# Splitting the first loads of q and k in two, with conversion, transposes and copies of the parts overlapped, in a fused sigmoid attention and SwiGLU kernel

## The chip, the cores and the metric

The kernel runs on one core of a Trainium2 chip. The metric is the device time of one execution in microseconds (us); lower is better. A kernel is compared with the kernel before only in the same rounds on the same chip.

## The reference

```python
def _attn_ref(q, k, v):                    # (8, 12, 448, 64) each
    S = q.shape[2]
    scores = q @ k.transpose(0, 1, 3, 2) / np.sqrt(q.shape[-1]) - np.log(S)
    return (1.0 / (1.0 + np.exp(-scores))) @ v

def _moe_ref(x, w_gate, w_val, w_out):     # x (3584, 768), d_ff 1536
    g = x @ w_gate
    return (g * (1.0 / (1.0 + np.exp(-g))) * (x @ w_val)) @ w_out
# reference = _moe_ref of the attention's output, heads joined, (3584, 768) float32
```

## The kernel before

The attention is cut into 24 tiles n of four heads, each into seven chunks c of keys. For a tile, q and k are loaded as float32, converted to bfloat16, transposed (for the first tiles on TensorE, by way of PSUM), multiplied into scores, put through a sigmoid on ScalarE (ACT), and multiplied with v ("PV"); three VectorE (DVE) instructions evacuate PV. Four PSUM tiles of two banks go round as a ring. The loads of v and of the weights convert to float16 on the way and are all issued by GpSimd (POOL).

```python
def load(n, which, eng=None):
    st = stg.tile([128, 2, S], FP32, tag="stg", name=f"st{which}_{n}")
    (eng or nc.sync).dma_start(out=st, in_=src_of(n, which))
    qkv_st[(n, which)] = st
# ... cut: cast(n, which, eng, lo, hi) converts chunks lo to hi of a loaded tile
load(0, 1, nc.scalar)                                  # first k
for n, which in ((0, 0), (1, 0), (1, 1), (2, 0), (2, 1), (3, 0), (3, 1)):
    load(n, which)                                     # SyncE's queue
# ... cut: sigmoid table
for i in range(9):                                     # warm-up of TensorE
    nc.tensor.matmul(out=ring[i % 4][:, i // 4 % 2, :], lhsT=warm[:, :128], rhs=warm, start=True, stop=True)
cast(0, 0, V)
cast(0, 1, nc.scalar, 0, 2)
cast(0, 1, G, 2, C)
trans_pe(0, ((0, 0, C), (1, 0, 2)), (V, nc.scalar))    # both into one PSUM tile
chunk(0, 0)                                            # scores and sigmoid
chunk(0, 1)
trans_pe(0, ((1, 2, C),))
cast(1, 0, G)
cast(1, 1, V)
load_v(0)                                              # on GpSimd's queue
w_load("g", 0)
# ... cut: more loads on GpSimd, chunks (0, 2) to (0, 4), trans_pe(1)
cast(2, 0, V)
cast(2, 1, V)
cast(3, 0, V)
cast(3, 1, V)
# ... cut: chunks (0, 5) to (1, 2)
pv(0)
# ... cut
for i, at in enumerate(((6, 4), (7, 0), (7, 4), (8, 0))):
    begin[at].append(lambda i=i: w_load("o", i))       # output weights
```

## Time and profile before

| | value | where it is read |
|---|---|---|
| time | 429.3 us (429.28 to 429.45) | three executions |
| span of the profiled execution | 426.6 us | page, first line |
| TensorE busy | 97% of the span | page, part 1 |
| first sigmoid starts | 7.95 us | timeline of ACT |
| v of tile 0 lands | 13.51 us | load records, issued 7.49, 6.0 us to landing |
| PV of tile 0 starts | 14.63 us | timeline of TensorE (PE) |
| last of the 21 head sigmoids starts | 26.32 us | timeline of ACT |

The timelines count from the first instruction; "landing" is the moment at which a load's semaphore tells that it is complete. Of the 10.7 us in which PE is idle, 5.6 lie in the first 30 us, where the change acts, and 4.4 after 394 us. From the last of the head's 21 sigmoids on, PE is dense, and every trace of this study without a new wait repeats that remainder to within 0.3 us (426.6 - 26.3 = 400.3 us here). The start of that sigmoid is therefore the figure by which to compare traces.

### The profile page before, as it was taken

How to read it: one execution, taken by the hardware profiler on the slowest of the kernel's cores; microseconds unless marked ns; L12 is line 12 of the kernel's file. 1: busy time of each engine (PE TensorE's matmuls, PEld its weight loads, DVE VectorE, ACT ScalarE, POOL GpSimd, SP SyncE). 2: the span in 40 equal slices, each digit the busy share in tenths (PEclk: the TensorE clock that was granted, in tenths of full speed). 3: DMA queues.
4: the chain of work that ended last, by engine and by line, in shares of the span. 5: the costliest groups of instructions: out<-in, count | busy, mean ns of one | idle time of the engine just before them, and what ended most of it. 6: DMA issues, size and time to landing. Idle time of an engine off the chain costs nothing.

```text
span 426.6 us, 7903 instructions
## 1 busy us (share of the span) xinstructions
PE 415.9 (97%) x3261; PEld 217.6 (51%) x3261; DVE 204.9 (48%) x337; ACT 211.9 (50%) x291; POOL 117.5 (28%) x167
## 2 busy tenths in 40 slices
PE   6899999999999999999999999999999999999995
PEld 2544544545555444545555544544555545555663
DVE  2726656555324555555323556555433356555322
ACT  4966885654624755656433755746433642222000
POOL 5564346401637346000345545000221100000000
PEclk8799999999999999999999999999999999999999
DMA  8999999995699997500298996600162300000234
GB/s 301 231 277 211 210 190 208 177 247 99 152 218 174 194 174 178 115 0 2 71 229 169 226 193 164 120 0 2 23 131 71 81 0 2 0 2 0 55 94 111
DMA packets 57796, 54.38 MB, mean 127 GB/s; under 512 B 35680, under 2 KB 52448, under 8 KB 57760
## 3 DMA queue, kind: packets, MB, share of 16 engines
q0 software_dynamic: 20896, 39.20, 40.9%
q1 hardware_dynamic: 36512, 14.13, 20.3%
q8 instruction: 25, 0.41, 0.4%
q10 hardware_dynamic: 352, 0.56, 0.4%
q14 instruction: 11, 0.09, 0.1%
HBM read 47.19 MB, written 11.01 MB: 136 GB/s over the span
## 4 chain that ended last, share of the span: by engine, by line
PE 91%; ACT 3%; DVE 2%; issue 1%; DMA 1%; ACTq 0%; DVEq 0%
PE ps_D L256 50%; PE ps_D L296 26%; PE ps_D L197 8%; PE ps_D L228 7%; ACT pt L215 2%; DMA st<-in_q_dram 1%; PE ps_D L171 1%; DVE t L273 1%; ACT s L271 1%; ACT pt L212 1%; DVE T L180 0%; DVE hT L277 0%; DVE xT L237 0%; DVE xT L245 0%; ACT xT L243 0%
## 5 line engine op out<-in xcount | busy, mean ns | idle before, releaser
L215 ACT ACTIVATE pt<-ps_D,sb_t 128x896 f16<-128x896 f32 x148 | 140.3, 1014 | 84.4 <-PE ps_D L197 84.2
L256 PE MATMUL ps_D<-xT,wg 128*128 128x448 f16 x576 | 126.9, 353 | 0.9 <-ACT pt L215 0.5
L256 PE MATMUL ps_D<-xT,wv 128*128 128x448 f16 x576 | 126.4, 352 | 0.0
L296 PE MATMUL ps_D<-wo,hT 128*128 128x384 f16 x672 | 111.8, 326 | 0.0
L273 DVE TENSOR_TENSOR t<-ps_D,s 128x448 f16<-128x448 f32 x96 | 59.9, 624 | 92.3 <-ACT s L271 92.0
L271 ACT ACTIVATE s<-ps_D 128x448 f16<-128x448 f32 x96 | 52.7, 549 | 90.6 <-PE ps_D L256 80.1
L296 PEld LDWEIGHTS <-hT 128*128 128x128 f16 x672 | 64.8, 98 | 46.4 <-issue 4.3
L256 PEld LDWEIGHTS <-wg 128*128 128x128 f16 x576 | 53.7, 98 | 58.5 <-issue 12.4
L256 PEld LDWEIGHTS <-wv 128*128 128x128 f16 x576 | 56.4, 98 | 52.8 <-issue 0.3
L327 DVE TENSOR_SCALAR osb<-ps_D 128x384 f32<-128x384 f32 x55 | 30.7, 558 | 74.2 <-PE ps_D L296 71.0
L277 DVE SCALAR_TENSOR_TENSOR hT<-ps_D,t 128x448 f16<-128x448 f32 x96 | 60.0, 625 | 10.4 <-DVE t L273 0.5
L337 POOL DMA_DIRECT2D out_dram<-osb x42 | 22.4, 537 | 146.1 <-DVE osb L327 146.1
L149 POOL CAST c<-st 128x896 bf16<-128x896 f32 (+1 forms) x42 | 38.8, 936 | 63.1 <-issue 29.6
L197 PE MATMUL ps_D<-T,T 64*64 64x448 bf16 x672 | 47.4, 367 | 2.3 <-ACT T L180 1.1
L228 PE MATMUL ps_D<-pt,v 64*64 64x448 f16 x672 | 36.2, 351 | 0.3 <-ACT pt L215 0.3
L197 PEld LDWEIGHTS <-T 64*64 64x64 bf16 x672 | 16.3, 107 | 25.9 <-issue 18.2
L237 DVE CAST xT<-ps_D 128x448 f16<-128x448 f32 x24 | 15.0, 625 | 29.8 <-PE ps_D L228 23.0
L245 DVE CAST xT<-ps_D 64x448 f16<-64x448 f32 x46 | 28.6, 622 | 0.7
L228 PEld LDWEIGHTS <-v 64*64 64x64 f16 x672 | 19.9, 108 | 13.0 <-issue 1.5
L212 ACT ACTIVATE pt<-ps_D,sb_t 128x448 f16<-128x448 f32 x40 | 23.0, 631 | 0.0
L140 POOL DMA_DIRECT2D v<-in_v_dram x24 | 17.7, 738 | 0.1
L135 POOL DMA_DIRECT2D st<-in_k_dram x20 | 14.7, 736 | 3.1 <-DMA wv<-in_moe_w_val_dram 3.1
(25 smaller groups left out, 59.6 us busy)
## 6 DMA issues: line engine op xcount, KB each, us to landing
st<-in_q_dram POOLq DMA_DIRECT2D x20, 448.0 KB, 4.8
st<-in_k_dram POOLq DMA_DIRECT2D x20, 448.0 KB, 7.0
out_dram<-osb POOLq DMA_DIRECT2D x42, 192.0 KB, 3.1
v<-in_v_dram POOLq DMA_DIRECT2D x24, 224.0 KB, 8.3
wg<-in_moe_w_gate_dram POOLq DMA_DIRECT2D x4, 576.0 KB, 14.4
wv<-in_moe_w_val_dram POOLq DMA_DIRECT2D x4, 576.0 KB, 14.6
wo<-in_moe_w_out_dram POOLq DMA_DIRECT2D x4, 576.0 KB, 14.7
out_dram<-osb SPq DMA_DIRECT2D x12, 192.0 KB, 2.7
```

The lines of the kernel that those rows point to most:

```text
L149: (eng.copy if eng is nc.scalar else eng.tensor_copy)(out=t.rearrange("p c h d -> p h c d"), in_=st.rearrange("p h (c d) -> p h c d", c=C) ...
L197: nc.tensor.matmul(out=sc[w * 64:(w + 1) * 64, h2, :S], lhsT=kt[r, w * 64:(w + 1) * 64], rhs=qt[r, :, w * 64:(w + 1) * 64], start=True, st ...
L212: nc.scalar.activation(out=pt[:, h2, :], in_=sc[:, h2, :S], func=SIGM, bias=sb_t, scale=qkscale), h2
L215: nc.scalar.activation(out=pt, in_=sc[:, :, :S], func=SIGM, bias=sb_t, scale=qkscale)
L228: nc.tensor.matmul(out=P[g:g + 64, h2, :S], lhsT=vt[r, h2, c * D:(c + 1) * D], rhs=pt[r, h2, :], start=(c == 0), stop=(c == C - 1),)
L245: nc.vector.tensor_copy(out=o, in_=i)
L256: nc.tensor.matmul(out=D.t[:, i, :S], lhsT=w16[f // FW][:, pr, cs], rhs=xT[(b, pr)], start=(pr == 0), stop=(pr == NP - 1),),
L271: D.read(nc.scalar.activation(out=s16, in_=D.t[:, 0, :S], func=SIGM), 0)
L273: D.read(nc.vector.tensor_tensor(out=t1, in0=D.t[:, 0, :S], in1=s16, op=MULT), 0)
L277: nc.vector.scalar_tensor_tensor(out=hT[(b // 2, f)][:, b % 2, :], in0=D.t[:, 1, :S], scalar=HSC, in1=t1, op0=MULT, op1=MULT),
L296: nc.tensor.matmul(out=D.t[:, half, :hw], lhsT=h[:, m * 128:(m + 1) * 128], rhs=wo16[f // FW][:, f % FW, half * hw:(half + 1) * hw], start ...
L327: nc.vector.tensor_scalar(out=osb[:, hs], in0=D.t[:, half, :hw], scalar1=HREC, scalar2=None, op0=MULT),
```

## The change

Its intent is that the first sigmoid should not wait for a whole q and k. Each comes as two loads; the first part is converted, transposed and copied while the second is still under way; q and k get their own PSUM tiles, so that ACT's copy of k need not follow VectorE's copy of q.

```diff
-    load(0, 1, nc.scalar)
-    for n, which in ((0, 0), (1, 0), ...):
+    QS, KS = 4, 2
+    load(0, 1, nc.scalar, 0, KS)        # k, chunks 0 and 1
+    load(0, 0, None, 0, QS)             # q, chunks 0 to 3
+    load(0, 0, None, QS, C)
+    load(0, 1, None, KS, C)             # rest of k, now on SyncE's queue
+    for n, which in ((1, 0), ...):
...
-    for i in range(9):
+    for i in range(8):
...
-    cast(0, 0, V)
-    cast(0, 1, nc.scalar, 0, 2)
-    cast(0, 1, G, 2, C)
-    trans_pe(0, ((0, 0, C), (1, 0, 2)), (V, nc.scalar))
+    cast(0, 1, nc.scalar, 0, KS)
+    cast(0, 0, V, 0, QS)
+    cast(0, 0, V, QS, C)
+    cast(0, 1, G, KS, C)
+    Dk, Dq = Banked(), Banked()         # a PSUM tile each
+    # ... cut: k part transposed, copied by ACT; two q parts transposed, copied by V
...
-    trans_pe(0, ((1, 2, C),))
+    trans_part(Dk, 1, 0, 1, KS, C, V, dk[1])()
```

More of the change, by code (lines that the diff above doesn't have):

```diff
@@ L131, in src_of, with load @@
         return (q, k, v)[which][b, 4 * j:4 * j + 4].rearrange("(h w) (p c) d -> (w p) h (c d)", w=2, c=C)
-    def load(n, which, eng=None):
-        st = stg.tile([128, 2, S], FP32, tag="stg", name=f"st{which}_{n}")
-        (eng or nc.sync).dma_start(out=st, in_=src_of(n, which))
-        qkv_st[(n, which)] = st
+    def load(n, which, eng=None, lo=0, hi=C):
+        whole = hi - lo == C
+        st = stg.tile(
+            [128, 2, (hi - lo) * D], FP32,
+            tag="stg" if whole else f"stg{which}_{lo}", bufs=None if whole else 1, name=f"st{which}_{n}_{lo}",
+        )
+        (eng or nc.sync).dma_start(out=st, in_=src_of(n, which)[:, :, lo * D:hi * D])
+        qkv_st[(n, which, lo)] = st
     def load_v(n):
@@ L143, in cast @@
     def cast(n, which, eng, lo=0, hi=C):
-        st = qkv_st[(n, which)]
-        if hi == C:
-            qkv_st.pop((n, which))
-        t = c16.tile([128, hi - lo, 2, D], BF16, tag="c16" if hi - lo == C else f"c16_{lo}", name=f"c16_{which}_{n}")
+        st = qkv_st.pop((n, which, lo))
+        whole = hi - lo == C
+        t = c16.tile(
+            [128, hi - lo, 2, D], BF16,
+            tag="c16" if whole else f"c16{which}_{lo}", bufs=None if whole else 1, name=f"c16_{which}_{n}_{lo}",
+        )
         q16[(n, which, lo)] = t
@@ L150, in cast @@
             out=t.rearrange("p c h d -> p h c d"),
-            in_=st.rearrange("p h (c d) -> p h c d", c=C)[:, :, lo:hi, :],
+            in_=st.rearrange("p h (c d) -> p h c d", d=D),
         )
@@ L161, in trans_dma, with trans_part, copy, trans_pe @@
             qT[(n, 0)] = d
-    def trans_pe(n, parts=((0, 0, C), (1, 0, C)), engs=(nc.vector, nc.vector)):
-        D2 = Banked()
+    def trans_part(D2, bank, n, which, lo, hi, eng, d):
+        t = q16.pop((n, which, lo))
         ps = D2.t.bitcast(BF16).rearrange("p w (c i) -> p w c i", c=8)
-        for i, (which, lo, hi) in enumerate(parts):
-            t = q16.pop((n, which, lo))
-            for c in range(hi - lo):
-                D2.write(
-                    nc.tensor.transpose(
-                        out=ps[:, i, c, :], in_=t[:, c].rearrange("p h d -> p (h d)"), identity=idn
-                    ),
-                    i,
-                )
-        for i, (which, lo, hi) in enumerate(parts):
-            tag = f"T{which}" if hi - lo == C else f"T{which}_{lo}"
-            d = qkT.tile([128, hi - lo, 128], BF16, tag=tag, bufs=None if hi - lo == C else 1, name=f"T{which}_{n}_{lo}")
-            copy = engs[i].copy if engs[i] is nc.scalar else engs[i].tensor_copy
-            D2.read(copy(out=d, in_=ps[:, i, :hi - lo, :]), i)
+        for c in range(hi - lo):
+            D2.write(
+                nc.tensor.transpose(
+                    out=ps[:, bank, c, :], in_=t[:, c].rearrange("p h d -> p (h d)"), identity=idn
+                ),
+                bank,
+            )
+        def copy():
+            f = eng.copy if eng is nc.scalar else eng.tensor_copy
+            D2.read(f(out=d, in_=ps[:, bank, :hi - lo, :]), bank)
             for c in range(lo, hi):
                 qT[(n, which, c)] = d[:, c - lo]
-            if which == 0:
-                qT[(n, 0)] = d
+        return copy
+    def trans_pe(n):
+        D2 = Banked()
+        ds = [qkT.tile([128, C, 128], BF16, tag=f"T{w}", name=f"T{w}_{n}") for w in range(2)]
+        for f in [trans_part(D2, w, n, w, 0, C, nc.vector, ds[w]) for w in range(2)]:
+            f()
+        qT[(n, 0)] = ds[0]
     pts = {}
@@ L384 @@
     V, G = nc.vector, nc.gpsimd
-    load(0, 1, nc.scalar)
-    for n, which in ((0, 0), (1, 0), (1, 1), (2, 0), (2, 1), (3, 0), (3, 1)):
+    QS, KS = 4, 2
[3 more added lines that the diff above has]
+    load(0, 1, None, KS, C)
+    for n, which in ((1, 0), (1, 1), (2, 0), (2, 1), (3, 0), (3, 1)):
         load(n, which)
     nc.scalar.activation(out=one.tile([128, 1], FP32, tag="tbl", name="tbl"), in_=sb_t, func=SIGM)
-    for i in range(9):
+    for i in range(8):
         nc.tensor.matmul(out=ring[i % 4][:, i // 4 % 2, :], lhsT=warm[:, :128], rhs=warm, start=True, stop=True)
-    cast(0, 0, V)
-    cast(0, 1, nc.scalar, 0, 2)
-    cast(0, 1, G, 2, C)
-    trans_pe(0, ((0, 0, C), (1, 0, 2)), (V, nc.scalar))
+    cast(0, 1, nc.scalar, 0, KS)
+    cast(0, 0, V, 0, QS)
+    cast(0, 0, V, QS, C)
+    cast(0, 1, G, KS, C)
+    dk = [qkT.tile([128, n, 128], BF16, tag=f"Tk{n}", bufs=1, name=f"Tk{n}") for n in (KS, C - KS)]
+    dq = qkT.tile([128, C, 128], BF16, tag="T0", name="T0_0")
+    Dk, Dq = Banked(), Banked()
+    trans_part(Dk, 0, 0, 1, 0, KS, nc.scalar, dk[0])()
+    copies = [
+        trans_part(Dq, 0, 0, 0, 0, QS, V, dq[:, :QS]),
+        trans_part(Dq, 1, 0, 0, QS, C, V, dq[:, QS:]),
+    ]
+    for f in copies:
+        f()
+    qT[(0, 0)] = dq
     def fetch(n):
```

## The prediction

> **What bounds the kernel now.** I read the page first, then the chain of work that ended last for the first 62 us, then the timeline of the first 26 us engine by engine, then the windows of the TensorE clock, last the landing of single loads.
>
> The page says where a change of the head can matter at all:
>
> ```profile
> span 426.6 us, 7903 instructions
> PE 415.9 (97%) x3261; PEld 217.6 (51%) x3261; DVE 204.9 (48%) x337; ACT 211.9 (50%) x291; POOL 117.5 (28%) x167
> ...
> PE   6899999999999999999999999999999999999995
> ```
>
> PE is busy 97% of the span. Only the first two of 40 slices (10.7 us each) and the last one have idle PE, so no change in the head can win more than the idle time there: 426.6 - 415.9 = 10.7 us in all, some of it at the end. A gain of 2% (8.6 us) would need nearly all of it.
>
> The chain of work, start and duration in us, shows what the first 7.5 us are made of:
>
> ```profile
> 0.74 4.32 DMA st<-in_q_dram
> ...
> 5.09 0.64 DVE c L149
> ...
> 5.77 0.58 PE ps_D L171 x7
> ...
> 6.37 0.64 DVE T L180
> ...
> 7.09 0.38 ACT T L180
> ...
> 7.52 0.57 PE ps_D L197 x8
> ```
>
> It is purely serial: q lands (5.06), is cast whole, transposed whole, copied whole; only then does ACT copy the first two chunks of k, though their transposes ended at 6.45. In the order of instructions that ACT copy waits for DVE as well as for PE, since both parts sit in one PSUM tile. Then come the first scores and, at 7.95, the first sigmoid. From there ACT is the bound (timeline of ACT and of PE, start and length, engine, line, operation, count, wait):
>
> ```profile
> 1.19 3.96 PE L390 MATMUL ps_D<-warm 128*128 128x512 bf16 x9 [1.19 <-DVE warm L62]
> ...
> 7.95 18.31 ACT L215 ACTIVATE pt<-ps_D,sb_t 128x896 f16<-128x896 f32 x20 [0.49 <-PE ps_D L197]
> ```
>
> Twenty sigmoids follow each other, one per 0.89 us (20 x 0.89 = 17.8 of the 18.3; one stall of 0.12 at 12.68). PE gets dense only when they are done. So a first sigmoid that starts X earlier moves the end by X, if nothing else in those 18 us ends later than the sigmoids.
>
> **What the Trainium skill says.** (1) "TensorE: Matmul & The Clock Gate", Part 1: the array runs at half clock until a free-running window of 3.4 us has been busy, and falls back after an idle one; Part 4 adds that transposes don't count as busy the same way. The trace agrees. The nine warm-up matmuls start 0.44 us apart, half rate, and the windows of that length read
>
> ```profile
> 4.97:8.38 3.41, 1.72 (x23) 0.93 (x22) 1.25 (x2) 1.21 (x3) 2.65 (x4) 1.00 1.05 390
> 8.38:11.79 3.41, 2.83 (x27) 1.85 (x26) 1.53 (x3) 3.41 (x5) 3.41 (x5) 0.50 1.06 382
> 11.79:15.21 3.42, 3.11 (x31) 1.14 (x33) 3.30 (x6) 3.30 (x4) 3.06 (x4) 0.50 1.29 208
> ```
>
> (length, then PE, PEld, DVE, ACT, POOL busy, granted clock, DMA share, GB/s): 1.72 us of PE work in the second window, then half clock for two windows. (2) "VectorE: DVE Perf Modes", "Why PSUM operands drop a tier": a copy out of PSUM in 16 bits runs at two elements a cycle at most. The trace has 0.622 us for 896 elements and 0.492 for 640, hence 0.51 ns per element and 0.167 us fixed, which is that rate. (3) "DMA: Bandwidth & Descriptors", Specifications: runs of 512 B or more are needed for line rate. The new parts have runs of 512, 768, 1024 and 1280 B (1792 before), so I expect no loss that matters; no run yet shows it.
>
> **The change part by part.**
>
> Loads. The bytes are the same, in another order: k part of 128 KB on ACT's queue, q parts of 256 and 192 KB, then 320 KB of k on SP's. Before, 917 KB of q and k landed by 5.36 at some 390 GB/s, with the flow beginning near 1.9. The windows of one us have 22, 194, 407, 393 GB/s from 1 to 5, so 0.22 MB are through by 3.0 and 0.62 by 4.0. The first 393 KB are then through at 3.45, all of q at 3.9, all of k at 4.75; with 0.3 for the completion (q's 5.06 against 4.75): first parts 3.4 to 3.8, second q part 4.2, rest of k 5.05. An estimate, from those rates.
>
> Casts. ACT's 256 elements took 0.41: done at 3.9. DVE's whole cast took 0.63; with the same split of fixed and per-element cost the parts take 0.43 and 0.36: done at 4.2 and 4.6. All this is before the warm-up ends.
>
> PE. It is in order, and eight warm-ups instead of nine end 0.43 earlier, near 4.72. This, and no longer the load, starts the transposes. Two of k and seven of q at 0.083 (0.58 / 7), the first two at half clock: k done 4.97, first four of q 5.30, last three 5.55.
>
> Copies. ACT's k copy of 0.37 runs from 5.0 to 5.37, beside DVE; its wait for DVE is gone in the order of the changed kernel, because Dk and Dq are separate tiles. DVE: 512 elements 0.43 (5.31 to 5.74), 384 elements 0.36 (to 6.11). First scores at 6.13, first sigmoid at 6.56 (7.52 to 7.95 was 0.43). **Gain at the first sigmoid: 7.95 - 6.56 = 1.39 us.** It is robust: the second q part may land as late as 5.05 without moving the second copy.
>
> Rest of k: cast on POOL 5.05 to 5.95, transposed behind the eight score matmuls from 6.7, copied by 7.65, third tile of scores at 8.1. The second sigmoid ends at 8.46, so ACT doesn't stall.
>
> Then v. The first weights of the PV product can't be loaded until v lands, and that doesn't move: it is issued by POOL behind a cast that waits for the second q (landed 6.56) and it stands behind 3.7 MB of loads that are all queued before it. In the load records (name, issuing queue, count, size, us to landing) the one issued at 7.49 has
>
> ```profile
> v<-in_v_dram POOLq DMA_DIRECT2D x1, 224.0 KB, 6.0
> ```
>
> so it landed at 13.51, and PE's timeline shows its first weight load at 13.74 and PV at 14.63, where it waited for the seventh sigmoid (ended 14.59). With everything 1.4 to 1.5 earlier that wait would end at 13.1, and v's landing takes its place: PV starts at 13.75, 0.88 earlier. It also spends 1.45 us instead of 0.57 in the half clock, which (if the clock keeps to 15.2) costs (1.45 - 0.57) / 2 = 0.44: PV ends 0.88 - 0.44 = 0.44 earlier, plus what rounding I allow, say 0.4 to 0.6. This matters because the path behind is tight: PV end 16.41, three DVE evacuations (16.53 to 18.44), scores at 18.49, ready at 18.92, sigmoid at 18.93, no slack. So of 1.4 us some 0.5 arrives if the clock is as before, and 0.9 if it is warm by then.
>
> Later landings have slack: the first wv at 21.39 (used 23.99), the second at 31.64 (used 34.38). Sum: -0.5 to -0.9, I take -0.7 from 429.3: 428.6 us.
>
> **Rivals.** (a) All of the 1.4 us arrives, 427.9: v lands earlier or its wait is covered by queued sigmoids, and PE stays warm. For: ACT holds three ready score tiles when PV starts, 2.7 us of work. Against: the tight evacuation path just told. (b) Nothing arrives, 429.3: v lands 0.3 to 0.5 later, since the split adds two loads and smaller descriptors ahead of it, and PV runs all cold. For: DMA is at share 1.05 from 3 us on. Against: the bytes are the same. (c) The clock: eight warm-ups fill the first window less, and the phase of the window is free. If PE stays cold from the start, transposes and scores double, some 0.5 to 1 us later, 429.3 or a bit more; if the denser 5 to 8 us avoid the cold stretch, (a). Against the latter: the added density is transposes mostly.
>
> **Range and chances.** The range runs from a bit beyond (a) to (b) with a little chip-to-chip difference: 427.6 to 429.5. Over 2% either way would need 8.6 us, more than the head holds for a gain, and no part of the change can cost as much: 0.01 each.
>
> **What would show it.** Right: first sigmoid near 6.6 instead of 7.95, ACT's k copy running beside DVE's, transposes starting as the last warm-up ends; v landing at 13.4 to 13.9, PV starting directly behind it, a stall of 0.4 to 0.7 us in ACT's row of sigmoids that the kernel before did not have; end of that row 0.5 to 0.9 earlier. Wrong: no new stall in ACT's row and the whole 1.4 at the end (then v was no bound), a first sigmoid later than 7 (parts landed late), or a clock that rises at another moment.

## The result, and the profile after

The changed kernel took 429.56 us (median of six executions, 428.12 to 430.31) against 429.4 (six, 429.28 to 429.48) of the kernel before. The ratio is 1.0002, 95% interval 0.9984 to 1.0020. Ratios here are the mean time of one kernel's fast runs over that of the other's of the same rounds, so not quite the ratio of the medians quoted. Repeated on two chips (after_again and after_third below), it came out at 1.0024 (1.0004 to 1.0043) and 1.0025 (1.0003 to 1.0048). So there is no gain, and perhaps a loss of a quarter of a per cent.

The head did become faster. This is the timeline of ACT in the changed kernel (start, length, engine, line, operation, tiles, count; in brackets the idle time before it and what ended it):

```profile
5.25 0.37 ACT L184 COPY Tk<-ps_D 128x256 bf16<-128x256 bf16 x1 [0.48 <-PE ps_D L176]
7.06 1.90 ACT L226 ACTIVATE pt<-ps_D,sb_t 128x896 f16<-128x896 f32 x2 [1.44 <-PE ps_D L208]
9.34 9.27 ACT L226 ACTIVATE pt<-ps_D,sb_t 128x896 f16<-128x896 f32 x10 [0.37 <-PE ps_D L208]
18.87 1.91 ACT L226 ACTIVATE pt<-ps_D,sb_t 128x896 f16<-128x896 f32 x2 [0.27 <-PE ps_D L208]
```

The copy of k no longer waits for VectorE, and the first sigmoid starts at 7.06 instead of 7.95. But the row, which before had one stall of 0.12, is now interrupted by 0.37 and 0.27 as well, and its last sigmoid starts at 26.23, only 0.09 earlier. The chain of work that ended last (start, length, what) says what it ran through:

```profile
2.27 5.37 DMA st<-in_q_dram
...
7.69 0.88 POOL c L156
8.57 6.22 DMA v<-in_v_dram
...
14.83 1.55 PE ps_D L239 x28
```

Where it went through q, its conversion, copy and scores before, it now goes through the load of the *second* q (tile 1, landed 7.64; 6.56 before), POOL's conversion of it, the issue of v behind that (8.57; 7.49 before), and v's landing at 14.79 (13.51 before).

The chain books all the time from issue to landing as the load's. The trace's packet records split it. v's first packet moves at 11.90, 3.3 us after its issue (before: 11.79, 4.3 us after), while the last packets of the q and k loads queued ahead of it start at 13.25 (before: 12.17). With two loads fewer ahead (after_v_wo below) the first packet came 1.8 us after the issue. So it is not the later issue that holds v but the loads ahead of it.

PE's timeline has the new wait in one line; the kernel before stands above, the changed one below, where the seventh sigmoid had ended at 14.11:

```profile
14.63 1.77 PE L228 MATMUL ps_D<-pt,v 64*64 64x448 f16 x28 [0.31 <-ACT pt L215]
14.83 1.52 PE L239 MATMUL ps_D<-pt,v 64*64 64x448 f16 x28 [0.99 <-DMA v<-in_v_dram]
```

One trace would be thin evidence, so here are all the traces. In each, the columns are read from the same three views. "Waits for" is what ended PE's idle time before PV of tile 0.

| kernel | first sigmoid | second q landed | v landed | PV starts | waits for | last head sigmoid | span |
|---|---|---|---|---|---|---|---|
| before | 7.95 | 6.56 | 13.51 | 14.63 | sigmoid | 26.32 | 426.6 |
| before_again | 8.11 | 6.53 | 13.52 | 15.13 | sigmoid | 26.81 | 427.0 |
| before_wo_first | 8.38 | 6.63 | 13.62 | 15.06 | sigmoid | 26.75 | 427.0 |
| before_v_wo | 8.06 | 6.53 | 11.22 | 14.74 | sigmoid | 26.42 | 426.8 |
| changed | 7.06 | 7.64 | 14.79 | 14.83 | v | 26.23 | 426.3 |
| after_again | 6.39 | 7.36 | 14.27 | 14.32 | v | 26.44 | 426.5 |
| after_third | 6.70 | 8.09 | 14.94 | 14.99 | v | 27.06 | 427.5 |
| after_wo_first | 6.63 | 8.07 | 14.96 | 15.01 | v | 27.08 | 427.2 |
| no_v_wait | 6.92 | 7.28 | (14.18) | 13.36 | sigmoid | 25.66 | 426.6 |
| after_v_wo | 6.80 | 7.68 | 12.44 | 13.25 | sigmoid | 26.73 | 427.0 |
| after_v2_wo | 6.70 | 7.62 | 12.56 | 13.48 | sigmoid | 26.91 | 427.1 |
| whole_loads | 7.59 | 6.57 | 13.54 | 14.19 | sigmoid | 25.87 | 426.1 |
| q_split | 7.44 | 6.94 | 13.89 | 13.93 | v | 25.62 | 425.8 |
| k_rest_act | 7.48 | 7.58 | 14.44 | 14.58 | sigmoid | 26.27 | 427.2 |

Take the first three rows as the head of before and the four from "changed" on as the head of after. The means of the first sigmoid are 8.15 and 6.70: a gain of 1.45. The means of v's landing are 13.55 and 14.74: a loss of 1.19. The last head sigmoid starts at 26.63 and 26.70: nothing is left.

### The profile page after: what moved, and what is told of

Read it like the earlier page. It is cut to its first block, busy times and chain, and to the rows that moved or that the text cites. A ratio compares the mean times of both kernels' runs of the same rounds, so it can differ in the third digit from the quotient of the medians.

```text
span 426.3 us, 7904 instructions
## 1 busy us (share of the span) xinstructions
PE 416.2 (98%) x3260; PEld 217.7 (51%) x3260; DVE 205.3 (48%) x339; ACT 211.9 (50%) x291; POOL 116.7 (27%) x167
## 4 chain that ended last, share of the span: by engine, by line
PE 90%; DMA 3%; ACT 3%; DVE 2%; issue 1%; SPq 0%; POOL 0%; DVEq 0%; ACTq 0%
PE ps_D L267 50%; PE ps_D L307 26%; PE ps_D L208 7%; PE ps_D L239 7%; DMA v<-in_v_dram 1%; ACT pt L226 1%; DMA st<-in_q_dram 1%; DVE t L284 1%; ACT s L282 1%; DVE xT L256 1%; ACT pt L223 1%; DVE xT L248 0%; DVE T L184 0%; SPq L140 0%; DVE hT L288 0%
## 5 line engine op out<-in xcount | busy, mean ns | idle before, releaser
L208 PE MATMUL ps_D<-T,T 64*64 64x448 bf16 x644 | 44.6, 360 | 1.2 <-DVE xT L256 0.6
L208 PEld LDWEIGHTS <-T 64*64 64x64 bf16 x644 | 15.4, 106 | 23.5 <-issue 18.0
## 6 DMA issues: line engine op xcount, KB each, us to landing
wg<-in_moe_w_gate_dram POOLq DMA_DIRECT2D x4, 576.0 KB, 14.3
wv<-in_moe_w_val_dram POOLq DMA_DIRECT2D x4, 576.0 KB, 14.6
wo<-in_moe_w_out_dram POOLq DMA_DIRECT2D x4, 576.0 KB, 14.3
```

What stands on the lines that cost most here:

```text
L208: nc.tensor.matmul(out=sc[w * 64:(w + 1) * 64, h2, :S], lhsT=kt[r, w * 64:(w + 1) * 64], rhs=qt[r, :, w * 64:(w + 1) * 64], start=True, st ...
```

## The experiments

The theories: **A**, v's landing takes the place of the wait removed. **B**, a cold array or a loss further on eats the gain. **C**, the split of the loads delays the row of transfers; within it **E1**, because most of k went to SyncE's queue behind q, and **E2**, because k is cut at all. **D**, a second bound near 101 us.

### after_again and before_again: how firm is the first trace?

Both kernels unchanged.

> The changed kernel once more, for a second trace and the spread. If the array's clock phase and the loads decide each execution, its times again spread over 1 us or more (428 to 430.5), the first sigmoid moves between 6.5 and 7.2 from trace to trace, and PV of tile 0 again starts within 0.1 us of v's landing (14 or later). If the first trace was an odd one, the spread is 0.3 us and v lands near 13.5.

> The control: the kernel before, with a second trace. Its six times lay within 0.2 us. Theory (v takes the place of the seventh sigmoid): again within 0.3 us at 429.3 to 429.5, v landing at 13.4 to 13.8, PV released by ACT at 14.6. If v's landing varies by itself, it shows here too.

Measured: after_again 430.35 us (428.32 to 431.06) and ratio 1.0024; before_again 428.9 (428.75 to 428.98, and one of 433.35). The first trace was no odd one: v again late, PV 0.05 behind it. The changed kernel spread as expected, a little past both ends (431.06 us, first sigmoid at 6.39). The control kept its narrow spread, apart from that one execution, but 0.5 us below the level that I expected, and PV was released at 15.13, not 14.6. A trace is always of one execution, and with the changed kernel this was the fastest of its six twice; the executions of 430 and more have no trace. The first trace of the kernel before is of a fast execution too (428.37 us, where the timed ones took 429.28 and more).

Here the clock comes in, though not as B had it. The windows of after_third show it (length, then busy time of PE, PEld, DVE, ACT and POOL, granted clock, share of the transfer engines, GB/s), and below them the same of before_again:

```profile
12.00:15.00 3.00, 0.40 (x8) 0.12 (x7) 1.86 (x3) 3.00 (x5) 3.00 (x5) 1.00 1.18 219
15.00:18.00 3.00, 3.00 (x42) 1.63 (x43) 1.06 (x2) 1.53 (x2) 1.48 (x2) 0.68 1.30 203
18.00:21.00 3.00, 3.00 (x41) 2.18 (x40) 2.53 (x6) 2.49 (x4) 1.04 (x2) 0.75 1.31 204
```

```profile
12.00:15.00 3.00, 2.62 (x26) 1.00 (x25) 2.88 (x5) 2.93 (x5) 2.81 (x4) 0.65 1.30 204
15.00:18.00 3.00, 2.27 (x40) 1.49 (x40) 2.17 (x4) 3.00 (x5) 0.83 (x2) 1.00 1.30 203
18.00:21.00 3.00, 2.68 (x44) 1.88 (x42) 2.54 (x6) 3.00 (x4) 0.71 (x1) 1.00 1.30 207
```

In after_third PE waits 2.33 us for v, is busy 0.40 of three us, and is then granted half clock exactly where PV and the scores behind it have to catch up: ACT idles about 1.5 of the next three us. The same happened in after_again (idle 1.47, then PV took 2.19 instead of 1.52). The kernel before is cold earlier and warm here. In these two traces the cold stretch adds to the wait. That the wait brings it on is not shown: in no_v_wait, after_v_wo and after_v2_wo below PV did not wait for v, and it ran at half clock all the same (2.43, 2.78 and 2.83 us).

### no_v_wait: does v's landing eat the gain?

```diff
+    v_now = one.tile([128, 2, S], FP16, tag="v_now", name="v_now")
+    V.memset(v_now, 0.05)
     load_v(0)
+    v16[0] = v_now        # PV of tile 0 reads this; wrong result on purpose
```

> The changed kernel, with PV of tile 0 reading a constant tile (wrong result on purpose); the load of v is still issued into its own tile, so the transfers are the same. Theory A (v's landing eats the gain of the head): PV starts behind the seventh sigmoid, near 13.9 to 14.1 where it was 14.83, the stall of 0.27 in ACT's row goes, and the time falls by 0.5 to 1.0 to 428.4 to 429.0. Theory B (a cold array, or loss further on, eats it): no change, 429.3 to 429.8.

Measured: 428.48 us (427.73 to 429.29), ratio to before 0.9987 (0.9974 to 1.0001). In the same rounds after_again had 1.0024 (1.0004 to 1.0043); the intervals don't meet. Taking v out of PV's way, with the same transfers, is worth 1.0024 - 0.9987, some 0.4% or 1.6 us. The two traced executions don't show this difference (428.40 and 428.32 us); it lies in those without a trace. PV started at 13.36, behind the seventh sigmoid, and the last head sigmoid at 25.66. Theory A holds, although what else the slow executions spent their time on was not seen. (The stall expected to go, 0.27, did not: PV ran at half clock in this trace, took 2.43, and ACT had a stall of 0.27 all the same.)

Its span of 426.6 doesn't fit, though: 25.66 + 400.3 would be 426.0. The waits of 98 to 104 us show why (who, for what: us in total, times, longest), and so does the chain of the same trace:

```profile
PE ps_D L307 <- DMA wo<-in_moe_w_out_dram: 0.3, 1, 0.3
```

```profile
69.74 16.52 DMA wo<-in_moe_w_out_dram
86.26 0.29 issue
86.55 15.18 DMA wo<-in_moe_w_out_dram
101.73 0.04 issue
101.77 4.39 PE ps_D L307 x26
```

The fourth load of the output weights lands at 101.73, when its first matmul is overdue: the ninth matmul of the second feed-forward product started at 101.14, and the tenth, the first to read it, at 101.77 instead of 101.30. (Some 0.4 had gone at 51 us, in a wait for VectorE of 0.58 where the other traces have 0.2.) This is a second bound, hidden in the kernel before: there the tenth matmul starts at 101.58 and the load landed at 101.26.

### whole_loads: is it the split of the loads?

```diff
-    load(0, 1, nc.scalar, 0, KS)
-    load(0, 0, None, 0, QS)
-    load(0, 0, None, QS, C)
-    load(0, 1, None, KS, C)
+    load(0, 1, nc.scalar)
+    load(0, 0)             # the parts are slices of the whole tiles
```

> The changed kernel with the two loads whole as before (k on ACT's queue, q on SP's); casts, transposes and copies stay in parts. Theory C (the split of the loads slows the row of transfers, so that v is issued and lands later): second q lands near 6.6, v at 13.5 instead of 14.8, first sigmoid at 7.4 to 7.6, PV at 14.1 to 14.3, time 428.9 to 429.2, 0.2 to 0.5 below the kernel before. If the split costs nothing in transfers: v again at 14.5 or later, time 429.4 or more.

Measured: second q at 6.57, v at 13.54, first sigmoid 7.59, PV 14.19, all as theory C said. The time was 428.91 us, ratio 0.9998 (0.9984 to 1.0012): equal to before, not the 0.2 to 0.5 below that I expected, though the trace had gained 0.5. Theory C holds for the transfers; the times don't decide it, since this interval and that of after_again (1.0004 to 1.0043) overlap. The overlap of conversion, transposes and copies alone gives about 0.6 us at the first sigmoid (7.59 against 8.15 in the mean).

### before_wo_first, after_wo_first: the second bound

```diff
-        begin[at].append(lambda i=i: w_load("o", i))
+        begin[at].insert(0, lambda i=i: w_load("o", i))
```

> The kernel before, with each of the four loads of the output weights issued ahead of the fetch it stood behind, not after it. Theory D (the fourth of them, landing at 98 to 102 us just as its first matmul is due at 101.1 to 101.6, is a second bound that sets the end in most timed executions): it lands before 98, the time falls by 0.3 to 0.8 against the kernel before of the same rounds and spreads less. Rival (D is an accident of single executions): the same within 0.2.

> The changed kernel with the same move of the output weights. Theory D: its slow executions of 430 to 431 (where the transfers, 0.7 to 1.0 later from the head on, bring the fourth output weight late) go; it falls by 1.2 or more to 428.1 to 428.8 and lies within 0.4 of the kernel before with the same move. If the slow executions come from the head alone (late v, cold array): it stays at 429.5 or more.

Measured: 428.76 us (428.17 to 429.72), ratio 0.9987 (0.9957 to 1.0016), and 429.23 (427.7 to 429.67), ratio 0.9988 (0.9957 to 1.0019). The fourth output weight landed at 91.87 and 94.75 in the two traces, so there the bound is gone; but the times can't tell, because two executions of the kernel before took 433 us in these rounds and widen the intervals. For the kernel before, my expectation of a gain is not borne out. The median of the changed kernel fell between my two expectations. None of its executions passed 429.7, where after_again and after_third each had three above 430.7; that would point to D in its slow executions, but it was another chip. And after_v_wo below, on the same chip and with the same move, had three executions of 430.3 to 430.7, which speaks against it. What is shown is the wait itself, in three traces: the tenth matmul is late by 0.5 in no_v_wait, 0.3 in after_third, and 0.8 in k_rest_act (at 102.30 behind a ninth at 101.35, where the usual step is 0.16). All three have the first k cut in two.

### after_v_wo, before_v_wo: an earlier v

```diff
-    for n, which in ((1, 0), ..., (2, 1), (3, 0), (3, 1)):
+    for n, which in ((1, 0), ..., (2, 1)):
         load(n, which)
...
     load_v(0)
+    load(3, 0, G)          # behind v on GpSimd's queue
+    load(3, 1, G)
```

plus the move of the output weights.

> The changed kernel with the move of the output weights, and the last two loads of q and k (tile 3) issued behind the first v on GpSimd's queue instead of ahead of it. Theories A and D together: v lands at 11.5 to 12.6, PV of tile 0 is released by the seventh sigmoid at 13.0 to 13.9, the row of sigmoids ends 0.5 to 0.9 earlier than in the changed kernel, the time is 427.4 to 428.0, 0.5 or more below both kernels with the output weights moved alone. If A is wrong: the same as those.

> The control for the last one: the kernel before with both moves. In it PV waited for the seventh sigmoid and not for v, so an earlier v should give nothing: within 0.2 of the kernel before with the output weights moved alone.

Measured: the control as expected, 428.75 us against 428.76 of before_wo_first: v landing 2.4 us earlier gives the kernel before nothing. But after_v_wo took 430.15 (ratio 1.0010, 0.9979 to 1.0042), a miss. v landed at 12.44 and PV began at 13.25 as expected. VectorE's timeline shows what happened then:

```profile
15.13 0.63 DVE L156 CAST c<-st 128x896 bf16<-128x896 f32 x1 [2.64 <-DMA st<-in_q_dram]
16.41 0.67 DVE L156 CAST c<-st 128x896 bf16<-128x896 f32 x1 [0.66 <-DMA st<-in_k_dram]
17.00 0.60 DVE L248 CAST xT<-ps_D 128x448 f16<-128x448 f32 x1
```

The conversions of tile 3 stand ahead of PV's evacuation in VectorE's order. Their loads, sent behind v, landed at 15.04 and 16.32, and the evacuation waited for them. I had moved a wait, not removed it.

### after_v2_wo: the same, mended

```diff
-    cast(3, 0, V)
-    cast(3, 1, V)
...
     pv(0)
+    cast(3, 0, V)          # behind the evacuation in VectorE's order
+    cast(3, 1, V)
```

> after_v_wo mended: in its trace VectorE's conversion of tile 3, whose loads now came behind v (landed 16.32), stood ahead of the evacuation of PV in VectorE's order and held it until 17.00. Here those two conversions come after that evacuation. Theory A: v lands near 12.5, PV starts at 13.0 to 13.4 released by the sigmoid, the evacuation follows PV at once, the scores behind it are due by 17.0 to 17.9, the row of sigmoids ends at 25.2 to 26.0 and the time is 0.5 to 1.2 below the changed kernel of the same rounds, 427.6 to 428.6. If A is wrong or the array's clock decides: no better than the changed kernel.

Measured: 428.76 us (427.76 to 428.99), ratio to before 0.9981 (0.9965 to 0.9997); after_third in the same rounds had 1.0025 (1.0003 to 1.0048). In means of the executions, 428.45 against 430.16 us. The mean is inside my range, the median just above it; the trace is not. Its last head sigmoid started at 26.91: PV ran at half clock (2.83 us), and the copies of tile 2, now behind the conversions of tile 3, gave ACT a stall of 0.41 at 21.13. Over all executions this version beats the changed kernel, but it holds three moves: of v, of the output weights and of the conversions. The output weights alone gave 0.9988 to before (after_wo_first, on another chip). That the earlier v is what pays is therefore not shown.

### after_third and q_split: which split costs?

```diff
-    load(0, 1, nc.scalar, 0, KS)
+    load(0, 1, nc.scalar)          # k whole on ACT's queue
     load(0, 0, None, 0, QS)
     load(0, 0, None, QS, C)
-    load(0, 1, None, KS, C)
```

> The changed kernel with the load of k whole on ACT's queue as before; only q comes in two loads. Theory E (it is the move of most of k behind q on SP's queue that delays the row of transfers): second q lands at 6.5 to 6.9, v at 13.5 to 13.8, first sigmoid at 6.9 to 7.1, PV at 13.8 to 14.1, row of sigmoids ends at 25.6 to 26.2, time 0.3 to 0.8 below the changed kernel. If each split costs alike: v at 14.0 or later and the time of the changed kernel.

> The changed kernel a third time, for the comparison with the other two on the same chip and a further trace: first sigmoid 6.4 to 7.1, v at 14.2 to 15.0, PV within 0.1 of it, row of sigmoids ends 26.2 to 27.1 (a trace of a slow execution, should it be one, 28 or more), time 0 to 1 above the kernel before.

Measured: q_split 428.44 us (427.58 to 429.5), ratio to before 0.9983 (0.9967 to 0.9999); after_third 430.04 (429.06 to 431.36), ratio 1.0025. ACT's timeline of q_split has the row whole again:

```profile
7.44 19.19 ACT L226 ACTIVATE pt<-ps_D,sb_t 128x896 f16<-128x896 f32 x21 [1.08 <-PE ps_D L208]
```

Its second q landed at 6.94, 0.4 later than before, where the changed kernel is 0.8 to 1.5 later. v still ended PV's wait, but by a hair: it landed at 13.89, and the seventh sigmoid ended at 13.88, so that the wait of 0.52 would have been as long without v. The first sigmoid was later than I had expected (7.44, not 6.9 to 7.1): the whole k landed at 5.18, ACT's conversion followed, and the transposes, k's first, began only at 5.66. The second part of q, landed at 5.74, came just in time behind them.

### k_rest_act: the queue or the cut?

```diff
     load(0, 1, nc.scalar, 0, KS)
+    load(0, 1, nc.scalar, KS, C)
     load(0, 0, None, 0, QS)
     load(0, 0, None, QS, C)
-    load(0, 1, None, KS, C)
```

> The changed kernel with the rest of k issued on ACT's queue behind the first part of k, not on SP's behind q; all four parts stay. Theory E1 (it is standing behind q on one queue that costs the changed kernel its microsecond): rest of k lands at 5.2 to 5.6 (6.1 to 6.5 in the changed kernel), second q at 6.7 to 7.1, v at 13.6 to 14.1, first sigmoid at 6.6 to 7.2, row of sigmoids ends at 25.3 to 26.0, time 0.5 to 1 below the kernel before, the best of all. Theory E2 (it is the split of k into runs of 512 and 1280 B itself): second q at 7.3 or later, v at 14.2 or later, time of the changed kernel, at or above the kernel before.

Measured: second q at 7.58, v at 14.44: E2's numbers, though the rest of k landed at 5.75. The queue is not the cause, the cut of k is, beside a cut q at least: neither k cut alone was run, nor a whole k with as many loads. The median of the five fast executions was 429.47 us (427.81 to 432.62; the sixth, 435.35, was slow), ratio 1.0011 (0.9953 to 1.0068), which says nothing either way. The windows of one us show the cost. Below are 3 to 7 us of the kernel before, of the changed kernel, and of q_split (the last two columns are the share of the transfer engines and GB/s):

```profile
3.00:4.00 1.00, 1.00 (x4) 0.31 (x3) 0.00 (x0) 0.00 (x0) 0.00 (x0) 1.00 1.05 407
4.00:5.00 1.00, 1.00 (x3) 0.15 (x1) 0.00 (x0) 0.00 (x0) 0.00 (x0) 1.00 1.05 393
5.00:6.00 1.00, 0.38 (x5) 0.23 (x5) 0.63 (x1) 0.41 (x1) 0.59 (x1) 1.00 1.05 398
6.00:7.00 1.00, 0.45 (x8) 0.27 (x5) 0.62 (x1) 0.00 (x0) 0.68 (x2) 1.00 1.06 392
```

```profile
3.00:4.00 1.00, 1.00 (x4) 0.32 (x3) 0.00 (x0) 0.00 (x0) 0.00 (x0) 1.00 1.11 361
4.00:5.00 1.00, 0.96 (x4) 0.18 (x3) 0.54 (x2) 0.41 (x1) 0.00 (x0) 1.00 1.05 314
5.00:6.00 1.00, 0.96 (x9) 0.80 (x8) 0.57 (x2) 0.37 (x1) 0.00 (x0) 1.00 0.98 314
6.00:7.00 1.00, 0.58 (x8) 0.20 (x8) 0.37 (x2) 0.00 (x0) 0.62 (x1) 1.00 1.03 357
```

```profile
3.00:4.00 1.00, 1.00 (x4) 0.32 (x3) 0.00 (x0) 0.00 (x0) 0.00 (x0) 1.00 1.02 371
4.00:5.00 1.00, 0.78 (x2) 0.00 (x0) 0.38 (x1) 0.00 (x0) 0.00 (x0) 1.00 1.08 387
5.00:6.00 1.00, 0.34 (x6) 0.34 (x6) 0.29 (x2) 0.42 (x2) 0.72 (x1) 1.00 1.08 396
6.00:7.00 1.00, 0.51 (x6) 0.27 (x4) 0.91 (x3) 0.35 (x1) 0.01 (x1) 1.00 1.04 375
```

The sums are 1590 KB before, 1346 KB in the changed kernel and 1529 KB in q_split, at nearly the same share. The engines are as busy and move less. 244 KB at 390 GB/s are 0.6 us; the rest of the delay of the second q is unevenness among the 16 engines, since a load lands with its slowest part. The sixteen signals that make up its landing came at 6.29 to 6.56 in the kernel before and at 6.41 to 7.64 in the changed one: the first is hardly late, the last by 1.1. The packet records give two components. First, a packet of 512, 768, 1024, 1280 and 1792 B takes 27, 36, 46, 55 and 74 ns (medians), so a row cut in two costs 8 ns more; two times 256 rows over 16 engines make 0.26 us for q and k together. Second, in 4 to 7 us the changed kernel has 31 packets of 120 to 570 ns, the kernel before 2, q_split none. Up to 16 us, packets of these loads that exceeded the norm of their size by over 60 ns numbered 22 to 29 in the five kernels with k whole and these loads in place (before, before_again, before_wo_first, whole_loads, q_split), and 36 to 51 in the six with k cut (changed, after_again, after_third, after_wo_first, no_v_wait, k_rest_act). What makes them, where k is read in two passes, stays open.

## Why the prediction was right or wrong

The kernel landed at the upper end of the range of 427.6 to 429.5 and above it (medians of 429.6, 430.4 and 430.0, beside 429.0 to 429.4 of before). That end of the range was rival (b), not the working, so that coming near it is luck. "Within 2%" was never in doubt. The point, a gain of 0.7, was wrong: the gain is nil.

- **The first sigmoid** was to be at 6.56, a gain of 1.39. The means are 6.70 and 1.45. The order of the parts, the end of the warm-up as what starts the transposes, and ACT's copy beside VectorE's are as told: in after_again the transposes start at 4.58, the copy of k at 4.99, the first scores at 5.96 (predicted 4.72, 5.0, 6.13). The changed trace is later (7.06) because the array was cold until 13.7 us: its nine transposes took 1.14, not 0.77, and its first eight score matmuls 0.96, not 0.57.
- **The landing of the parts** was too early in every term: rest of k at 6.08 to 6.32 instead of 5.05. The first sigmoid withstood it, as the prediction said it would for q.
- **The step that failed** is "v doesn't move". I let v depend on the bytes ahead of it, which are the same, and on the second q at 6.56. With k cut the second q came 0.8 to 1.5 later, as did the loads behind it, and v, last in that row, landed at 14.3 to 15.0, not 13.4 to 13.9. Its issue came later too, but did not hold it. The sentence on which it rested, "I expect no loss that matters" from cutting the runs to 512 to 1280 B, was the error.
- **The wait that takes the place** of the sigmoid's was named rightly, and no_v_wait shows it. The new stall in ACT's row, put at 0.4 to 0.7, was 0.27 in the first trace and 1.0 to 1.5 in the other three. It should have cost 0.5 to 0.9 of 1.4; with v's delay it cost all. Of the rivals, (b), a later v with nothing arriving, is what happened, with a delay of 0.8 to 1.5 instead of 0.3 to 0.5; I had argued against it with "the bytes are the same".
- **The clock** was thought to cost 0.44 within PV. PV did take longer in after_again and after_third (2.19 and 1.81 us, against 1.52 at full clock), and the cold stretch went on behind it.
- **Not foreseen**: the fourth output weight at 101 us. I had checked the later landings only up to the second wv at 31.64 us, and said they have slack. Whether the executions of 430 to 431 us come from this bound stays open: no trace fell on one, and after_v_wo had such executions although in its trace this weight landed at 99.19, in time.

Two versions beat both kernels, by 0.2% against the kernel before and 0.4% against the changed one in the same rounds: q_split, which cuts q alone, and after_v2_wo. The upper ends of their intervals, 0.9999 and 0.9997, are close to no gain at all.

## What to carry to other kernels

Before a path is shortened, look up the next thing that its consumers wait for, and ask whether the change can delay that one: here a load that nobody waited for had 1.1 us of slack, less than the head gained. Equal bytes are not equal time: to cut a load is to add packets, and here whatever was queued behind it came later, though another engine had issued it. Moving a load back moves a wait to every instruction that stands behind its consumer on an in-order engine.

## What the Trainium skill lacked or had wrong

- "DMA: Bandwidth & Descriptors", Specifications, gives 512 B as the size from which transfers run at line rate. Here a 512 B packet took 27 ns and one of 1792 B 74 ns (19 against 24 bytes per ns), and cutting the rows of k into 512 and 1280 B, beside those of q, brought the flow from 393 to 398 down to 314 GB/s for two us. The page does tell elsewhere of a fixed cost of each packet. That k read in two passes gets more slow packets (36 to 51 against 22 to 29) is on no page I read.
- "TensorE: Matmul & The Clock Gate", the table "Why this matters for your kernels", warns of idle gaps over about 3 us. Half clock also followed gaps of 1.47 and 2.33 us in stretches sparse otherwise (granted 0.50 and 0.68 over 15 to 18 us), and in no_v_wait 3.4 us in which PE was busy 1.80, with no gap over 0.51. A figure for how sparse a stretch may be is missing. That the phase of the window varies from run to run, as the page says in Part 1, these traces confirm: with the same eight warm-up matmuls the nine transposes took 0.77 us in one and 1.14 us in another.
- "VectorE: DVE Perf Modes", "Why PSUM operands drop a tier", agreed and lacked nothing: the two copies, estimated at 0.43 and 0.36, took 0.43 and 0.35 (0.69 together, since they overlap).
